# RWKV-6 attention with an MLP on one core: r-u-k products of round 2 as tasks between MLP steps, GpSimd's chain there one slot earlier, and the first MLP's second products in runs of three

## The chip, the cores and the metric

The kernel runs on one core of a Trainium2 chip. Its time is the device time in microseconds, the median over runs. A core has TensorE (PE, matrix products, with a weight load PEld beside it), VectorE (DVE), ScalarE (ACT), GpSimd (POOL) and SyncE, whose queue (SPq) issues nearly all DMAs here. Each engine works through its own instructions in order and waits for semaphores of the others.

## The reference

Four batches, eight heads of 48, 768 steps. An RWKV-6 recurrence runs over the steps, and its output, with the heads side by side (384 wide), goes through a layer norm and an MLP (384 to 1536 to 384) with a residual:

```python
for t in range(S):
    cur = np.einsum('bhd,bhe->bhde', u[None] * kt, vt)
    y[:, :, t] = np.einsum('bhd,bhde->bhe', rt, state + cur)
    state = wt[:, :, :, None] * state + np.einsum('bhd,bhe->bhde', kt, vt)
...
xn = (x - mu) / np.sqrt(var + 1e-06) * g_ln
ch = np.maximum(xn @ w_ch1, 0.0) @ w_ch2
return x + ch
```

The step's own term, `r . (u * k)` times `v`, is what the code calls the r-u-k product: `own_products` multiplies r, k and u, `own_sums` sums over a head's 48 numbers, `own_term` multiplies the sums with v.

## The kernel before

**Rounds, units, levels.** The work is cut into 8 rounds (4 batches, 2 halves of 384 steps). A round has two units of four heads each, so round 2 has units 4 and 5, and round 3 has units 6 and 7. Within a round the recurrence is solved in six levels (`lev` 0 to 5) that double the span each time. A level of a unit is `quads` (PE, products of r and k into `a_ps`), then `grow` (DVE, multiplies r and k by decays, `rkT<-rkT,tot` or `rkT<-rkT,wT`) and `keep` (DVE, into `A`). Level 5 is followed by `ends` (PE transposes `kn_ps`, ACT copies `kn`). In the next round `states` makes `kv` on PE and `s` on DVE, `exchanged` copies `sx` on ACT, and `outputs` makes `y` on PE and adds `vo` on DVE into `x`.

**The MLP beside it.** The MLP of a finished round is a generator, `mlp`, of 24 steps: 12 make a block of the hidden layer each (`h_ps` on PE, `h` on ACT), 12 make parts of the second product (`o_ps`), with three products to a step. When a block's 12 products are done, DVE adds `x` into `o` and a DMA writes it. PSUM has two buffers (`ps_m`) for `h_ps` and `o_ps` together. The first MLP takes its first two blocks of rows together (`groups`), all others one after another. Its weights are converted on the way: `begin` (ACT), `shifted` and `added` (DVE) handle 24 parts, and `converted(n)` makes sure that n parts are issued.

**The order.** The loop over `rnd` and `lev` is the written order of all work. Each (`rnd`, `lev`) is a slot, `slot = (rnd - 1) * NLEV + lev`. A slot does some work at once and collects the rest in `tasks`. `fill(UNTIL[slot], tasks)` then spreads the tasks evenly among the MLP steps up to the number `UNTIL[slot]`: with m tasks and n steps, a step follows whenever (i + 1) * n // m grows. PE, ACT, DVE and POOL (all wrapped in `InOrder`) keep the written order. So does `SPO` on the DMA queue, where an instruction is pinned behind the one written just before it on that queue; plain `SP` instructions may be moved ahead when their inputs are ready and a buffer is free.

**The operations around the change.** From round 3 on the units take the level-0 term another way: `load_before` fetches k and v one step earlier into the two old `nat_w` buffers (`i` 0 for k, 1 for v), `own_products` multiplies that k by r as well (`nat_w<-nat_w,nat_r`), `own_sums` sums it too (`next`), and `own_term` has three multiplications for one. `stage` loads `w_runs`, `k_runs` and `r_runs` into a ring of four raw buffers, `squares` transposes them on DVE. `totals` makes products of decays (`tot`, `decay`), on POOL for the rounds spoken of here. The product tile `rk` has one buffer, which `own_products` fills and `own_sums` frees. All operations of the compute engines show as L49 in the profile, since a helper records them; the DMA queue's lines are those of `load` (L125), `stage` (L163), `load_before` (L174), `load_v` (L186), `load_vx` (L192) and the write of `out` (L743).

Of the kernel before, what the change touches and what calls it, by code (L numbers as in the profile page):

```python
# [52 lines left out]
def kernel(  # L53
# [19 lines left out]
    P = 128  # L73
# [11 lines left out]
    NLEV = 6  # L85
# [243 lines left out]
    def converted(n):  # L329
        while joined < n:  # L330
            join()
# [377 lines left out]
    def mlp(rnd):  # L709
        b, f0 = rounds[rnd]  # L710
        x, xT, name = xs[b, f0], xTs[rnd], f"{b}_{f0}"
        hs = []
        for f in range(FC):
            converted(KC * (f * P // WC + 1))
            ps = ps_m.tile([P, RN], F32, tag="m", name=f"h_ps{name}_{f}")
            for kc in range(KC):
                PE.matmul(
                    ps, w1_sb[:, kc, ts(f, P)], xT[:, kc, :], start=kc == 0, stop=kc == KC - 1
                )
            hs.append(ph.tile([P, RN], F32, tag="h", name=f"h{name}_{f}"))  # L720
            ACT.activation(out=hs[f], in_=ps, func=AF.Relu)
            yield

        groups = ((0, 1), (2,)) if rnd == 0 else ((0,), (1,), (2,))
        at = 0
        for group in groups:
            ps = {
                i: ps_m.tile([P, H, D], F32, tag="m", name=f"o_ps{name}_{i}") for i in group
            }
            for f in range(FC):  # L730
                converted(len(parts) - FC + f + 1)
                for i in group:
                    PE.matmul(
                        ps[i].rearrange("p h d -> p (h d)"), hs[f][:, ts(i, P)],
                        w2_sb[:, f, :], start=f == 0, stop=f == FC - 1,
                    )
                    at += 1
                    if at % KC == 0 and f < FC - 1:
                        yield
            for i in group:  # L740
                o = p2.tile([P, H, D], F32, tag="o", name=f"o{name}_{i}")
                DVE.tensor_tensor(out=o, in0=ps[i], in1=x[:, i], op=ALU.add)
                SP.dma_start(  # L743
                    out=out[b, ds(f0 * RN + i * P, P), :].rearrange("t (h d) -> t h d", d=D),
                    in_=o,
                )
            yield
# [36 lines left out]
    def each(f, *ranges):  # L784
        calls = [()]
        for r_ in ranges:
            calls = [c + (x,) for c in calls for x in r_]
        return [lambda c=c: f(*c) for c in calls]
# [8 lines left out]

    FIRST = 3
    odd = const.tile([P, 1], F32, name="odd")

    def take(eng, q):

        own_products(q, eng)
        own_sums(q)


    (u0, u1), new = units_of(0), units_of(1)
# [91 lines left out]
    for rnd in range(1, NR + 1):  # L899
        old, now, new = units_of(rnd - 1), units_of(rnd), units_of(rnd + 1)  # L900
        if rnd == 1:
            old = []
        for lev in range(NLEV):
            slot = (rnd - 1) * NLEV + lev
            if rnd == 2:

                for q in old if lev < 2 else []:
                    (states, outputs)[lev](q)
                    if lev or q == old[-1]:
                        mlp_step()  # L910
            elif old and lev < 2 * U:
                (states if lev < U else outputs)(old[lev % U])
                if lev >= U and now:
                    mlp_step()
            for q in now:
                if slot and (lev or rnd < FIRST):
                    quads(q, lev)
            for which in ("rk",) if lev < NLEV - 1 else "kr":
                for q in now:
                    grow(q, lev, which)  # L920
            if now:
                if rnd == 1 and lev == 0:
                    totals(rnd, DVE)
                keep(rnd, lev)
            tasks = []
            if rnd == 1:
                if lev < 2:
                    tasks += each(load, new, "kr"[lev], [SPO])
                if lev == 2:
                    SPO.dma_start(  # L930
                        out=u_bc,
                        in_=bass.AP(
                            tensor=u.tensor, offset=u.offset, ap=[[0, P], [D, H], [1, D]]
                        ),
                    )
                    tasks += each(load_v, now, [SPO])
                if lev == 3:
                    tasks += each(load_vx, now, [SPO])
                if lev in (4, 5):
                    own_term(now[lev - 4], POOL)  # L940
            if rnd == 2 and lev == 0:
                tasks += each(load_v, now)
                DVE.tensor_reduce(
                    out=odd, in_=ident.rearrange("p (q two) -> p q two", two=2)[:, :, 1],
                    axis=AX.X, op=ALU.add,
                )
            if rnd == 2 and lev == 2:
                for q in now:
                    take(DVE, q)
                    tasks += each(load, new[q % U :][:1], "kr")  # L950
            if rnd == 2 and lev in (3, 4):
                tasks += each(own_term, now[lev - 3 :][:1], [POOL])
            if rnd > 2 and lev == 1:
                tasks += each(load, new, ["kr"])
            first = 3 if rnd == 2 else 1
            if rnd > 1 and new and first - 1 <= lev < first + 3:
                m = lev - first
                turns = [(new, "w"), (new[:1], "kr"), (new[1:], "kr")]
                if m >= 0:
                    tasks += each(squares, *turns[m], pairs)  # L960
                if m < 2:
                    tasks += each(stage, *turns[m + 1], pairs)
            if rnd == 2:
                if lev == 0:
                    tasks += each(exchanged, old)
                if lev == 1:
                    tasks += [lambda: moments(1), lambda: norm(1)]
                if lev == 2:
                    tasks += each(turned_x, [1], range(KC))
            elif old and lev < U:  # L970
                tasks += each(exchanged, [old[lev]])
            if lev == 3 and rnd > 1:
                for q in now:
                    load_vx(q)
                for q in new:
                    load_v(q)
                if new:
                    load_before(new[0], k, 0)
                    load_before(new[0], v, 1)
                if rnd > 2:  # L980
                    moments(rnd - 1)
                    tasks = each(norm, [rnd - 1]) + tasks
            if lev == 4 and rnd > 2:
                tasks += each(turned_x, [rnd - 1], range(KC))
            if lev == 4 and rnd > 1:
                tasks += each(own_products, new[:1], [POOL])
            if lev == NLEV - 1:

                if now:
                    mlp_step()  # L990
                if rnd >= 2 and new:
                    own_sums(new[0])
                if rnd >= 2:
                    tasks += each(load_before, new[1:], [k], [0])
                    tasks += each(own_term, new[:1], [POOL])
                    tasks += each(load_before, new[1:], [v], [1])
                    tasks += each(own_products, new[1:], [POOL])
                    tasks += each(own_sums, new[1:]) + each(own_term, new[1:], [POOL])
                    if new:
                        tasks += each(totals, [rnd + 1], [POOL])  # L1000
                if now:
                    tasks = mixed(
                        tasks,
                        each(ends, now, pairs) + each(finish, [2, 2, 4])
                    )
                if rnd == 1:
                    tasks = [join] * JOINS[lev] + tasks + each(totals, [rnd + 1], [POOL])
            if rnd == 1 and lev < NLEV - 1:

                n = (1, 2, 2, 1, 0, 0)[lev] * NP  # L1010
                tasks += mixed(
                    [begin] * BEGINS[lev], [join] * JOINS[lev], ahead[:n],
                    each(product_sums, now) if lev == 1 else [],
                )
                del ahead[:n]
            fill(UNTIL[slot], tasks)
            if lev == (2 if rnd == 2 else 4) and old:
                mlps.append(mlp(rnd - 1))
# [32 lines left out]
```

## Time and profile before

| | us |
|---|---|
| median of 9 runs | 565.66 |
| lowest and highest | 563.68 and 567.8 |
| the profiled execution, its own time | 566.1 |
| its span in the profile | 564.4 |
| TensorE busy in it | 547.2 (97%) |
| VectorE, ScalarE, GpSimd busy | 332.1, 168.8, 133.6 |

The span covers the instructions; the device time has 1.7 us more around them. A line of a timeline gives the start and the length in us, the engine, the operation, what it writes and reads, shapes, how many were merged, and in brackets the idle time before it with what ended it. Small matrix products are pipelined, so a busy TensorE need not be TensorE at its peak. The granted clock is the share of TensorE's full clock that it was given. A product of full precision is two records on PE.

### The profile page before, as it was taken

Reading aid. Unit: us, or ns where it says so; the run is one execution under the profiler, and the core shown is the slowest. Engines: PE = TensorE matmul, PEld = TensorE weight load, DVE = VectorE, ACT = ScalarE, POOL = GpSimd, SP = SyncE. Lnnn points to the kernel's source line nnn. Section 1 sums busy time; section 2 is a strip of 40 time slices with the busy share of each in tenths; the row PEclk is TensorE's granted clock in tenths of the full one; section 3 lists DMA queues with packets and bytes.
Section 4 is the critical chain, followed back from the end, with each engine's and each line's share of the span. In section 5 each row is a group of like instructions: output and inputs, shape, how many; then the busy total and the mean of one; then the engine's idle time right before and its main releaser. Section 6 shows DMA issues by size and latency. Waiting matters only on the chain.

```text
span 564.4 us, 18202 instructions
## 1 busy us (share of the span) xinstructions
PE 547.2 (97%) x7898; PEld 358.5 (64%) x7898; DVE 332.1 (59%) x654; ACT 168.8 (30%) x363; POOL 133.6 (24%) x157
## 2 busy tenths in 40 slices
PE   8999998998889999999999999999999999999997
PEld 6776665665555666666666666666666666665554
DVE  4889998769767785757386655666572611130000
ACT  3576877502250015201421026201521025202200
POOL 6040010205184019301590029021640000000000
PEclk9899999999997999999999999999999999999999
DMA  9948887245466464636463546545200000000000
GB/s 233 194 127 168 189 218 185 57 95 100 131 150 140 123 130 118 133 113 141 96 138 100 134 113 140 115 120 116 58 1 2 31 15 1 2 29 15 0 15 28
DMA packets 141552, 56.64 MB, mean 100 GB/s; under 512 B 124448, under 2 KB 130720, under 8 KB 141472
## 3 DMA queue, kind: packets, MB, share of 16 engines
q1 hardware_dynamic: 139600, 54.88, 41.9%
q8 instruction: 62, 1.02, 0.7%
q10 hardware_dynamic: 1872, 0.59, 0.4%
q14 instruction: 18, 0.15, 0.1%
HBM read 48.66 MB, written 4.72 MB: 95 GB/s over the span
## 4 chain that ended last, share of the span: by engine, by line
PE 82%; DVE 8%; ACT 3%; DMA 2%; issue 2%; SPq 1%; POOL 0%; DVEq 0%; ACTq 0%; POOLq 0%
PE o_ps L49 33%; PE h_ps L49 27%; PE a_ps L49 9%; PE y L49 4%; DVE rkT L49 3%; DVE w_sb L49 2%; PE kv L49 2%; PE kn_ps L49 2%; ACT rest L49 1%; DMA nat_r<-in_r_dram 1%; PE xT_ps L49 1%; PE own_ps L49 1%; PE k_ps L49 1%; PE r_ps L49 1%; DVE A L49 1%
## 5 line engine op out<-in xcount | busy, mean ns | idle before, releaser
L49 PE MATMUL o_ps<-w_sb,h 128*128 128x384 f32 x576 | 199.8, 496 | 1.0 <-ACT h L49 1.0
L49 PE MATMUL h_ps<-xT,w_sb 128*128 128x384 f32 x576 | 196.4, 491 | 2.6 <-DVE o L49 1.4
L49 PEld LDWEIGHTS h_ps<-xT,w_sb 128*128 128x128 f32 x576 | 105.6, 190 | 70.4 <-DVE o L49 2.0
L49 PEld LDWEIGHTS o_ps<-w_sb,h 128*128 128x128 f32 x576 | 106.4, 192 | 67.6 <-ACT h L49 2.3
L49 DVE TENSOR_TENSOR rkT<-rkT,tot 128x768 f32<-128x768 f32 (+1 forms) x96 | 77.4, 847 | 27.8 <-issue 17.6
L49 ACT ACTIVATE h<-h_ps 128x384 f32<-128x384 f32 x96 | 46.9, 488 | 142.6 <-PE h_ps L49 142.4
L49 PEld LDWEIGHTS a_ps<-rkT 48*64 48x64 f32 x4128 | 65.7, 136 | 24.2 <-issue 13.1
L49 PE MATMUL a_ps<-rkT 48*64 48x32 f32 x4128 | 70.9, 221 | 4.0 <-DVE rkT L49 3.9
L49 DVE TENSOR_TENSOR o<-o_ps,x 128x384 f32<-128x384 f32 x24 | 13.3, 555 | 95.8 <-PE o_ps L49 95.7
L49 POOL TENSOR_TENSOR vo<-v,own 128x576 f32<-128x576 f32 x16 | 19.5, 1223 | 104.5 <-DVE own L49 62.2
L49 ACT ACTIVATE rstd<-mv,eps 128x3 f32<-128x3 f32 x8 | 2.4, 296 | 133.5 <-DVE mv L49 133.5
L49 DVE SCALAR_TENSOR_TENSOR s<-s,decay,kv 128x48 f32<-128x48 f32 x160 | 29.3, 258 | 18.9 <-PE kv L49 18.9
L49 POOL TENSOR_TENSOR nat_w<-nat_w,nat_r 128x576 f32<-128x576 f32 x10 | 14.4, 1436 | 102.8 <-DMA nat_w<-in_v_dram 101.8
L49 DVE COPY_PREDICATED A<-mask,a_ps 128x768 f32<-128x768 int8 x32 | 38.3, 1198 | 0.0
L49 DVE TENSOR_TENSOR x<-y,vo 128x288 f32<-128x288 f32 x32 | 13.2, 453 | 35.4 <-PE y L49 35.4
L49 ACT ACTIVATE xT<-xT_ps,g_sb 128x384 f32<-128x384 f32 x24 | 13.6, 579 | 48.4 <-PE xT_ps L49 48.4
L49 DVE TENSOR_TENSOR rkT<-rkT,wT 128x768 f32<-128x768 f32 x16 | 24.9, 1590 | 0.9 <-PE a_ps L49 0.8
L49 DVE TENSOR_REDUCE own<-rk 128x12 f32<-128x576 f32 x12 | 9.0, 750 | 23.2 <-POOL rk L49 23.2
L49 DVE TENSOR_SCALAR w_sb<-w_sb 128x384 f32<-128x384 f32 (+1 forms) x48 | 20.4, 425 | 0.8
L49 DVE STREAM_TRANSPOSE rkT<-r_runs 128x384 f32<-128x384 f32 x20 | 15.6, 841 | 3.7 <-DMA r_runs<-in_r_dram 3.7
L49 PEld LDWEIGHTS y<-v,A 64*64 64x64 f32 x384 | 12.8, 134 | 7.6 <-issue 4.4
L49 POOL TENSOR_TENSOR tot<-wT 128x768 f32<-128x768 f32 x6 | 12.4, 2072 | 20.7 <-DVE rkT L49 20.7
(88 smaller groups left out, 541.1 us busy)
## 6 DMA issues: line engine op xcount, KB each, us to landing
raw<-in_moe_w_ch_dram SPq DMA_DIRECT2D x24, 384.0 KB, 3.8
w_runs<-in_w_dram SPq DMA_DIRECT2D x79, 70.0 KB, 2.0
k_runs<-in_k_dram SPq DMA_DIRECT2D x79, 70.0 KB, 1.9
r_runs<-in_r_dram SPq DMA_DIRECT2D x79, 70.0 KB, 2.0
v<-in_v_dram SPq DMA_DIRECT2D x48, 96.0 KB, 2.9
out_dram<-o SPq DMA_DIRECT2D x24, 192.0 KB, 2.5
nat_r<-in_r_dram SPq DMA_DIRECT2D x42, 96.0 KB, 3.3
nat_k<-in_k_dram SPq DMA_DIRECT2D x42, 96.0 KB, 3.4
```

The costliest lines, as they stand in the source:

```text
L49: return lambda *args, **kw: self.tc.keep_in_program_order(f(*args, **kw))
```

## The change

It has three parts. In the first MLP the second products of two row blocks no longer alternate from product to product: three products of one block run, then three of the other. In round 2, level 2, the r-u-k products and sums of units 4 and 5 become tasks in front of the loads that overwrite their inputs, and the loads of unit 6's shifted k and v and of v are written there, the shifted ones through the pinned queue. And in round 2 POOL's chain for units 6 and 7 is written one level earlier: unit 6's products in level 3, its sums and term and unit 7's products in level 4, where they were in levels 4 and 5. For later rounds the chain's code is shared and its order kept.

```diff
-        at = 0
         for group in groups:
...
-            for f in range(FC):
-                converted(len(parts) - FC + f + 1)
+            for f0_ in range(0, FC, KC):
+                converted(len(parts) - FC + f0_ + KC)
                 for i in group:
-                    PE.matmul(
-                        ps[i].rearrange("p h d -> p (h d)"), hs[f][:, ts(i, P)],
-                        w2_sb[:, f, :], start=f == 0, stop=f == FC - 1,
-                    )
-                    at += 1
-                    if at % KC == 0 and f < FC - 1:
+                    for f in range(f0_, f0_ + KC):
+                        PE.matmul(
+                            ps[i].rearrange("p h d -> p (h d)"), hs[f][:, ts(i, P)],
+                            w2_sb[:, f, :], start=f == 0, stop=f == FC - 1,
+                        )
+                    if f < FC - 1 or i != group[-1]:
                         yield
...
-    def take(eng, q):
-
-        own_products(q, eng)
-        own_sums(q)
...
             if rnd == 2 and lev == 2:
                 for q in now:
-                    take(DVE, q)
+                    tasks += each(own_products, [q], [DVE]) + each(own_sums, [q])
                     tasks += each(load, new[q % U :][:1], "kr")
+            if rnd == 2 and lev == 2:
+                tasks += each(load_before, new[:1], [k], [0], [SPO]) + each(load_v, new)
+                tasks += each(load_before, new[:1], [v], [1], [SPO])
             if rnd == 2 and lev in (3, 4):
                 tasks += each(own_term, now[lev - 3 :][:1], [POOL])
...
             if lev == 3 and rnd > 1:
                 for q in now:
                     load_vx(q)
-                for q in new:
-                    load_v(q)
-                if new:
-                    load_before(new[0], k, 0)
-                    load_before(new[0], v, 1)
                 if rnd > 2:
+                    for q in new:
+                        load_v(q)
+                    if new:
+                        load_before(new[0], k, 0)
+                        load_before(new[0], v, 1)
                     moments(rnd - 1)
                     tasks = each(norm, [rnd - 1]) + tasks
             if lev == 4 and rnd > 2:
                 tasks += each(turned_x, [rnd - 1], range(KC))
-            if lev == 4 and rnd > 1:
+
+            chain = 3 if rnd == 2 else 4
+            if rnd > 1 and new and lev == chain:
                 tasks += each(own_products, new[:1], [POOL])
+            if rnd > 1 and new and lev == chain + 1:
+                if lev < NLEV - 1:
+                    tasks += each(own_sums, new[:1])
+                else:
+                    own_sums(new[0])
+                tasks += each(load_before, new[1:], [k], [0])
+                tasks += each(own_term, new[:1], [POOL])
+                tasks += each(load_before, new[1:], [v], [1])
+                tasks += each(own_products, new[1:], [POOL])
             if lev == NLEV - 1:
 
                 if now:
                     mlp_step()
-                if rnd >= 2 and new:
-                    own_sums(new[0])
                 if rnd >= 2:
-                    tasks += each(load_before, new[1:], [k], [0])
-                    tasks += each(own_term, new[:1], [POOL])
-                    tasks += each(load_before, new[1:], [v], [1])
-                    tasks += each(own_products, new[1:], [POOL])
                     tasks += each(own_sums, new[1:]) + each(own_term, new[1:], [POOL])
                     if new:
                         tasks += each(totals, [rnd + 1], [POOL])
```

## The prediction

> **What bounds the kernel now.** I read the page first, then the time TensorE (PE) waited, then the chain of waits and the timelines of PE, VectorE (DVE), GpSimd (POOL) and the DMA queue (SPq) between 86 and 176 us, where both edits lie.
>
> ```profile
> span 564.4 us, 18202 instructions
> PE 547.2 (97%) x7898; PEld 358.5 (64%) x7898; DVE 332.1 (59%) x654; ACT 168.8 (30%) x363; POOL 133.6 (24%) x157
> ```
> PE is busy for 97% of the span: a gain can only come out of the 17 us in which it idles, or out of stretches in which it runs slowly. From 182 to 400 us the table by stretches shows it busy all the time, so whatever is won before 182 reaches the end whole.
>
> The first idle piece is in the first MLP, where its second products (`o_ps`) begin (PE's timeline):
> ```profile
> 87.86 2.20 PE L49 MATMUL h_ps<-xT,w_sb 128*128 128x384 f32 x6 [0.50 <-ACT h L49]
> 90.13 0.91 PE L49 MATMUL o_ps<-w_sb,h 128*128 128x384 f32 x2
> 92.01 3.49 PE L49 MATMUL o_ps<-w_sb,h 128*128 128x384 f32 x10 [0.97 <-ACT h L49]
> ```
> One product is two records. The first product of block 0 runs; the first of block 1 writes the other PSUM buffer, which ScalarE (ACT) has still to empty of the last `h_ps`: 0.97 us.
>
> The second idle region is the end of round 2 (PE's timeline again):
> ```profile
> 149.20 2.20 PE L49 MATMUL h_ps<-xT,w_sb 128*128 128x384 f32 x6
> 152.66 0.87 PE L49 MATMUL kn_ps<-ident,rkT 128*128 128x128 f32 x6 [1.25 <-DVE rkT L49]
> 165.63 0.91 PE L49 MATMUL kv<-v,kn 64*64 64x48 f32 x48
> 168.81 0.90 PE L49 MATMUL a_ps<-rkT 48*64 48x32 f32 x48 [2.27 <-DVE rkT L49]
> 170.86 1.50 PE L49 MATMUL a_ps<-rkT 48*64 48x32 f32 x48 [1.15 <-DVE rkT L49]
> ```
> PE waits for DVE three times. The 2.27 and 1.15 us are slack: work that PE does later before them costs nothing until they are used up. Behind them PE runs at half clock (stretches; the column after POOL's is the granted clock):
> ```profile
> 166.00:170.00 4.00, 1.44 (x87) 1.24 (x77) 4.00 (x9) 1.24 (x3) 3.91 (x3) 0.98 0.55 157
> 170.00:173.00 3.00, 2.14 (x49) 1.87 (x50) 2.89 (x12) 0.00 (x0) 2.62 (x5) 0.50 0.55 103
> 173.00:176.00 3.00, 3.00 (x6) 1.69 (x5) 3.00 (x7) 0.86 (x2) 0.40 (x2) 0.50 0.87 165
> 176.00:179.00 3.00, 3.00 (x9) 1.67 (x8) 3.00 (x5) 0.00 (x0) 2.57 (x2) 0.89 0.74 143
> ```
> The 18 `o_ps` records from 172.37 take 8.16 us in the chain of waits; 18 such records take 6.00 from 242.50. The half clock costs 2.16 us.
>
> What sets DVE there (timelines of DVE, SPq and POOL):
> ```profile
> 151.36 0.85 DVE L49 STREAM_TRANSPOSE rkT<-r_runs 128x384 f32<-128x384 f32 x1 [0.94 <-DMA r_runs<-in_r_dram]
> 152.07 1.92 DVE L49 TENSOR_TENSOR rkT<-rkT,tot 128x384 f32<-128x384 f32 x4
> 153.91 0.74 DVE L49 TENSOR_REDUCE own<-rk 128x12 f32<-128x576 f32 x1
> 155.83 1.55 DVE L49 STREAM_TRANSPOSE rkT<-k_runs 128x384 f32<-128x384 f32 x2
> 161.59 0.75 DVE L49 TENSOR_REDUCE own<-rk 128x12 f32<-128x576 f32 x1 [0.79 <-POOL rk L49]
> 164.03 0.75 DVE L49 TENSOR_REDUCE next<-nat_w 128x12 f32<-128x576 f32 x1 [1.69 <-POOL nat_w L49]
> ```
> ```profile
> 153.51 3.96 SPq L163 DMA_DIRECT2D r_runs<-in_r_dram  x8
> 157.58 2.22 SPq L174 DMA_DIRECT2D nat_w<-in_k_dram  x3
> ```
> ```profile
> 162.57 1.43 POOL L49 TENSOR_TENSOR nat_w<-nat_w,nat_r 128x576 f32<-128x576 f32 x1 [1.01 <-DMA nat_w<-in_k_dram]
> ```
> DVE's last wait (164.03) is for POOL, POOL's is for the shifted k of unit 7, and that load stands behind 32 DMAs that SPq issues back to back from 141.35.
>
> **Runs of three.** The instructions are the same, three to a step. Block 1's first product moves behind three of block 0: 90.13 + 3 x 0.65 (1.94 for a step) = 92.07, against 92.01 when its buffer is free. The 0.97 us go. The step now needs the third converted part at once; by 90 us DVE has joined 18 parts and the step needs 15, the later steps 18, 21 and 24 at about 96, 103 and 107, joined by 88.8, 95.8 and 103.7. No new wait. From 92 to 119.55 PE waits only once more (0.30, for ACT), and `grow` at 120.58 waits for PE; from there DVE, SPq and DMA hang on one another. So all of it moves: -0.97. Bounds: 0 if DVE's conversions (no idle over 0.52 us from 83 to 103) took over, -0.97 otherwise; I take -0.97, since each row above leaves room.
>
> **Round 2's products between steps.** In slot 8 the list has 19 tasks and three MLP steps, and a step comes after tasks 7, 13 and 19. All four tasks on DVE are among the first six, and the only DVE operation of the three steps (the `o` add at 135.46) is in the last: DVE's order is what it was, so 0, and the 1.37 us that PE waits for this `o` at 136.07 stay. The loads of k and r wait for the same products as before: 0.
>
> **Unit 6's shifted loads.** They are issued at 55 to 58 (k) and at 66.6 and 103 (v) before; now k is pinned behind the r load of unit 7, whose last DMA is issued at 136.71. SPq is idle from 138.01 to 141.35; three such DMAs take 1.55: they fit. Landing: the same kind takes 2.9 us at the median, so about 141. POOL now runs unit 6's products before `vo` of unit 5: they need r of unit 6 (about 136), so 136.2 to 140.2, then the shifted product to 142.7; before, 142.36. `vo` of unit 5 (1.15) moves behind, beside `grow` at 143.24: up to +1.2 us on DVE (a 0.96 multiply took 2.16 beside POOL at 137.5), which DVE's waits for DMAs (1.10, 0.93, 0.94) hide; if they were gone it would cost all of it. The early loads' place at 55 to 103 frees 6 DMAs, of which no engine waits for one: 0.
>
> **POOL's chain one slot ahead.** `own_sums` of unit 6 moves from behind the four level-5 multiplies to before them, but behind the `r_runs` transposes that end at 152.21. That is 155.83 - 153.91 = 1.92 us put in front of the multiplies that PE waits for at 152.66. They then start at 153.99, beside POOL's `vo` chain, which now starts at 153. Bounds for the first of them: 0.53 alone, 1.2 at the ratio 2.16/0.96; I take 1.0 from the ratio at 135.93 (two multiplies of 0.96 in 3.74). PE's transposes: 155.0 for 152.66, +2.35; behind them 2.27 + 1.15 us of slack. DVE finishes the multiplies at about 157.6 and the four transposes at about 160.6, inside its wait of 1.86.
>
> The gain meant here does not come: the k load of unit 7 stays behind `r_runs` on SPq (its buffer comes free after the last transpose, which frees the raw buffer of the last `r_runs` first), so the shifted product stays at 162.57 and `next` at 164.03. Of DVE's waits 0.79 us merge into the 1.69. The `s` and `grow` operations keep their times, PE's `a_ps` too: 0. Rounds after 2 keep the order of every engine: 0.
>
> **The clock.** PE's idle time moves: 151.34 to 155.0 (3.7 us) for 1.25, and the 2.27 is gone. In the trace half clock came at 169.9 for 6.8 us, after a stretch with idle pieces of 2.27 and 1.15 us; pieces of 1.37 (134.7) and 1.25 (151.4) brought none. I expect it to follow the new gap in three cases of four, and not at 170, where 1.15 us is left. There it falls on work with 1.15 us of slack. If it lasts 3.4 us (as at 23 us in the trace) it costs 1.7 - 1.15 = 0.55, if 6.8, 2.25; I take 0.75 x 0.55 = +0.4, and -2.16 for the old place.
>
> [...]
>
> Sum against the profiled execution (566.1, span 564.4 and 1.7 around it; the median 565.66 lies 0.44 below): 566.1 - 0.97 - 2.16 + 0.4 = 563.4.
>
> **The rivals.** 0.3% (1.70 us) is about what a measurement of this kernel can tell; faster means below 563.96, slower above 567.36.
> - Forecast, 0.50: 563.4, its own range 562.3 to 564.9; 0.37 of it below 563.96.
> - The half clock stays as dear (two windows at the new gap, or again at 170): 566.1 - 0.97 = 565.1. For it: the 48-row products before 172 are light work. 0.22, same.
> - DVE's conversions take the 0.97 over and the clock price stays: 565.7. 0.07, same.
> - POOL's lead pays: the k load of unit 7 gets in front of `r_runs` without holding it, 0.79 + 1.69 go: 563.4 - 2.5 = 560.9. Against it: SPq's order. 0.08, faster.
> - Slower: unit 6's k load, no longer early, is queued behind `k_runs` and `r_runs` (149.71). The last of three lands about 153.9; POOL's product 1.45, DVE's reduce and scale 1.3, so the multiplies start near 157.2 and PE at 157.7: +5.0, less 2.27 of slack = +2.7, and a longer gap saves no clock: 566.1 - 0.97 + 2.7 = 567.8. It decides once that load lands later than 152.07 - 1.45 = 150.6. For it: nothing pins `k_runs` behind it. 0.13.
>
> Range 562.0 to 567.2: leaves out 0.08 below and about 0.1 above. Faster 0.45, same 0.42, slower 0.13.
>
> **What would show it.** `o_ps` opens with six records and no wait at 90. DVE's `own` stands before the four 128x384 multiplies; PE's `kn_ps` wait is 3 to 4 us; the 2.27 before `a_ps` is gone; `next` still waits for POOL and that for `nat_w`; the granted clock is 1.00 from 170 to 177. I am wrong if half clock is still there, or if `next` no longer waits.

## The result, and the profile after

The changed kernel takes 562.44 us (median of 17 runs, 559.41 to 565.13), the kernel before 566.05 in the same measurement (54 runs). The ratio is 0.9938, 95% interval 0.9921 to 0.9954: faster by 0.6%, about 3.5 us. The profiled execution took 563.73 us, its span is shorter by 2.4 us:

```profile
span 562.0 us, 18190 instructions
PE 547.3 (97%) x7898; PEld 359.4 (64%) x7898; DVE 336.0 (60%) x654; ACT 169.2 (30%) x363; POOL 136.2 (24%) x157
```

The span alone misleads here. At about 23 us, long before the first edit acts at 90 us, PE ran at half clock for 10.2 us in this execution and for 3.4 us in the one of before, and the first `o_ps` began 2.51 us later (92.64 against 90.13). So I compare by stretches between marks on PE: *o1* is the first `o_ps` of the first MLP, *M2* the first `a_ps` of round 2 at level 1, *o3* the first `o_ps` of round 3's MLP steps (before: 172.30), *y3* the first `y` of round 3. From y3 to the end of PE's last instruction, all profiles but one take 380.43 us (that one 380.54), so what differs lies ahead of y3.

| us | before | after | difference |
|---|---|---|---|
| start to o1 | 90.13 | 92.64 | +2.51 |
| o1 to M2 | 29.42 | 28.37 | -1.05 |
| M2 to o3 | 52.74 | 51.09 | -1.65 |
| o3 to y3 | 8.16 | 6.00 | -2.16 |

The first MLP, PE's timeline:
```profile
90.34 2.20 PE L49 MATMUL h_ps<-xT,w_sb 128*128 128x384 f32 x6 [0.75 <-ACT h L49]
92.64 4.14 PE L49 MATMUL o_ps<-w_sb,h 128*128 128x384 f32 x12
```
Twelve records of `o_ps` (six products) stand without a wait; the 0.97 us behind the first product are gone.

The end of round 2, PE's timeline:
```profile
155.52 1.33 PE L49 MATMUL kn_ps<-ident,rkT 128*128 128x128 f32 x6 [2.67 <-DVE rkT L49]
157.04 0.88 PE L49 MATMUL kn_ps<-ident,rkT 128*128 128x128 f32 x3 [0.18 <-DVE rkT L49]
157.71 2.84 PE L49 MATMUL h_ps<-xT,w_sb 128*128 128x384 f32 x6
...
169.86 0.92 PE L49 MATMUL kv<-v,kn 64*64 64x48 f32 x48
170.60 1.57 PE L49 MATMUL a_ps<-rkT 48*64 48x32 f32 x96
172.10 6.07 PE L49 MATMUL o_ps<-w_sb,h 128*128 128x384 f32 x18
```
Both waits before `a_ps` (2.27 and 1.15 us) are gone, the one before `kn_ps` has grown from 1.25 to 2.67, and the 18 `o_ps` are at full speed. The stretches of the same profile (the granted clock is the column after POOL's) show where the half clock went:
```profile
155.00:157.00 2.00, 1.33 (x6) 0.93 (x6) 2.00 (x4) 0.59 (x2) 1.77 (x2) 0.70 0.57 156
157.00:160.00 3.00, 2.96 (x8) 2.05 (x9) 3.00 (x2) 0.85 (x2) 2.92 (x3) 0.63 0.63 157
...
170.00:173.00 3.00, 3.00 (x147) 2.69 (x146) 2.89 (x13) 0.46 (x1) 2.59 (x5) 1.00 0.72 150
173.00:176.00 3.00, 3.00 (x11) 1.75 (x10) 3.00 (x5) 0.86 (x2) 0.00 (x0) 1.00 0.82 153
```
It begins at 155.8, lasts 3.4 us and stretches six `kn_ps` from 0.87 to 1.33 and six `h_ps` from 2.10 to 2.84.

DVE's timeline, then POOL's, then the DMA queue's:
```profile
137.38 3.02 DVE L49 TENSOR_TENSOR rkT<-rkT,tot 128x768 f32<-128x768 f32 x2
...
153.05 0.70 DVE L49 TENSOR_REDUCE own<-rk 128x12 f32<-128x576 f32 x1
...
154.92 5.33 DVE L49 TENSOR_TENSOR rkT<-rkT,tot 128x384 f32<-128x384 f32 x4
...
163.72 0.75 DVE L49 TENSOR_REDUCE next<-nat_w 128x12 f32<-128x576 f32 x1
```
```profile
138.07 1.52 POOL L49 TENSOR_TENSOR rk<-nat_k,nat_r 128x576 f32<-128x576 f32 x1 [2.47 <-DMA nat_r<-in_r_dram]
...
143.65 1.43 POOL L49 TENSOR_TENSOR nat_w<-nat_w,nat_r 128x576 f32<-128x576 f32 x1 [1.98 <-DMA nat_w<-in_k_dram]
...
162.24 1.45 POOL L49 TENSOR_TENSOR nat_w<-nat_w,nat_r 128x576 f32<-128x576 f32 x1 [0.72 <-DMA nat_w<-in_k_dram]
```
```profile
138.71 2.51 SPq L49 DMA_DIRECT2D nat_w<-in_k_dram  x3
...
142.07 3.89 SPq L163 DMA_DIRECT2D k_runs<-in_k_dram  x8
...
158.20 1.49 SPq L174 DMA_DIRECT2D nat_w<-in_k_dram  x3
```
Four things to see. The two level-3 multiplies of `grow` take 3.02 us for 3.74. `own` stands ahead of the level-5 multiplies, and these take 5.33 us for 1.92. DVE doesn't wait for POOL any more, and `next` runs at 163.72. Counted from M2, `k_runs` begins on SPq at 21.07 instead of 21.80.

### The profile page after: what moved, and what is told of

The parts are those of the page before. It is cut to its first block, busy times and chain, and to the rows that moved or that the text cites. A ratio compares the mean times of both kernels' runs of the same rounds, so it can differ in the third digit from the quotient of the medians.

```text
span 562.0 us, 18190 instructions
## 1 busy us (share of the span) xinstructions
PE 547.3 (97%) x7898; PEld 359.4 (64%) x7898; DVE 336.0 (60%) x654; ACT 169.2 (30%) x363; POOL 136.2 (24%) x157
## 3 DMA queue, kind: packets, MB, share of 16 engines
q8 instruction: 62, 1.02, 0.8%
## 4 chain that ended last, share of the span: by engine, by line
PE 85%; DVE 7%; SPq 3%; DMA 2%; ACT 2%; issue 1%; ACTq 0%; DVEq 0%
PE o_ps L49 33%; PE h_ps L49 29%; PE a_ps L49 9%; PE y L49 4%; DVE w_sb L49 3%; PE kv L49 2%; PE kn_ps L49 2%; DVE rkT L49 2%; DMA nat_r<-in_r_dram 1%; SPq L163 1%; PE xT_ps L49 1%; PE own_ps L49 1%; PE k_ps L49 1%; PE idle L49 1%; PE r_ps L49 1%
## 5 line engine op out<-in xcount | busy, mean ns | idle before, releaser
L49 PE MATMUL o_ps<-w_sb,h 128*128 128x384 f32 x576 | 197.4, 492 | 0.1
L49 DVE TENSOR_TENSOR rkT<-rkT,tot 128x768 f32<-128x768 f32 (+1 forms) x96 | 82.0, 895 | 30.7 <-issue 17.6
L49 ACT ACTIVATE h<-h_ps 128x384 f32<-128x384 f32 x96 | 46.9, 489 | 143.8 <-PE h_ps L49 143.6
L49 PE MATMUL kn_ps<-ident,rkT 128*128 128x128 f32 x96 | 14.6, 288 | 3.8 <-DVE rkT L49 2.9
L49 PEld LDWEIGHTS kn_ps<-ident,rkT 128*128 128x128 f32 x96 | 11.5, 146 | 9.5 <-DVE rkT L49 3.6
```

The source lines that it names most:

```text
L49: return lambda *args, **kw: self.tc.keep_in_program_order(f(*args, **kw))
```

## The experiments

Each kernel is read by the same marks, in one profile for each row. "Half clock" gives start and length of the stretch that falls between 150 and 180 us.

| kernel | o1 to M2 | level-3 multiplies | M2 to `k_runs` on SPq | `k_runs` to unit 7's `next` | M2 to o3 | o3 to y3 | M2 to y3 | half clock |
|---|---|---|---|---|---|---|---|---|
| before | 29.42 | 3.74 | 21.80 | 22.68 | 52.74 | 8.16 | 60.91 | 169.9, 6.8 |
| after | 28.37 | 3.02 | 21.07 | 21.65 | 51.09 | 6.00 | 57.10 | 155.8, 3.4 |
| runs of three alone | 28.40 | 3.74 | 21.80 | 22.54 | 52.44 | 7.16 | 59.61 | 172.0, 3.4 |
| all but runs of three | 29.43 | 1.82 | 21.19 | 21.65 | 51.67 | 6.00 | 57.68 | 154.2, 3.4 |
| changed, sums back | 28.39 | 3.03 | 21.08 | 22.26 | 51.60 | 8.48 | 60.08 | 167.7, 6.8 |
| before, zeros ahead of `a_ps` | 29.42 | 3.75 | 21.80 | 23.01 | 52.47 | 6.00 | 58.47 | none |
| changed, zeros ahead of `kn_ps` | 28.41 | 3.02 | 21.05 | 22.81 | 51.76 | 7.39 | 59.15 | 171.7, 3.4 |
| before, level-2 tasks and pinned loads | 29.43 | 3.74 | 21.77 | 23.09 | 52.53 | 6.00 | 58.53 | 155.1, 3.4 |
| before, unit 6's products early | 29.42 | 1.82 | 19.87 | 22.81 | 50.94 | 7.77 | 58.71 | 167.2, 6.8 |
| sums back, totals early | 28.41 | 3.03 | 21.39 | 23.35 | 51.14 | 7.64 | 58.78 | 172.6, 3.4 |
| the parts that paid, and zeros | 28.39 | 3.03 | 21.25 | 22.67 | 50.40 | 6.00 | 56.40 | none |
| changed, loads unpinned | 28.41 | 1.82 | 19.87 | 21.72 | 49.26 | 6.00 | 55.26 | none |
| the same, second profile | 28.38 | 3.03 | 21.08 | 22.79 | 51.53 | 6.00 | 57.53 | 155.2, 3.4 |
| changed, second profile | 28.38 | 1.82 | 21.24 | 21.80 | 51.39 | 6.00 | 57.39 | 155.5, 3.4 |

**Runs of three alone.** The diff's first hunk by itself, on the kernel before:

```diff
-            for f in range(FC):
-                converted(len(parts) - FC + f + 1)
+            for f0_ in range(0, FC, KC):
+                converted(len(parts) - FC + f0_ + KC)
                 for i in group:
+                    for f in range(f0_, f0_ + KC):
...
```

> Only the runs of three, the rest as before. Theory (the wait for the second PSUM buffer goes and nothing takes it over): o_ps opens without its 0.97 us wait, and the kernel gains about 1.0 us against before; half clock still falls near 170 us. Rival (DVE's conversions take it over, and all of the change's gain lies in round 2): within 0.3 us of before.

Measured: o1 to M2 is 28.40, so 1.02 us are won and kept; every kernel that has this part shows 28.4, every one without it 29.4. M2 to y3 came out 1.3 us shorter too, though no edit lies there: the half clock lasted 3.4 us instead of 6.8. By the runs the median is 564.45 against 565.85, ratio 0.9989 (0.9968 to 1.001), which cannot tell 1 us from nothing. The stretch can.

**All but the runs of three.** The changed kernel with the old loop over `f` and `i`:

```diff
-            for f0_ in range(0, FC, KC):
-                converted(len(parts) - FC + f0_ + KC)
+            for f in range(FC):
+                converted(len(parts) - FC + f + 1)
                 for i in group:
-                    for f in range(f0_, f0_ + KC):
...
```

> Only round 2's part (tasks, pinned loads, GpSimd's chain one slot ahead), the second products alternate as before. Theory (PE's gap moves from 167 to 152, where there is slack, and half clock with it): 2 to 3 us faster than before, kn_ps waits about 3 us, no half clock near 170. Rival (the gain is the runs of three and little else): within 0.5 us of before.

Measured: 563.53 against 565.85, ratio 0.9965 (0.9943 to 0.9988). The half clock behind `a_ps` is gone and one of 3.4 us is at 154.2. Round 2's part is the larger one.

**Changed, but unit 6's sums back behind the level-5 multiplies.**

```diff
-            if rnd > 1 and new and lev == chain + 1:
-                if lev < NLEV - 1:
-                    tasks += each(own_sums, new[:1])
-                else:
-                    own_sums(new[0])
+            if rnd > 1 and new and lev == NLEV - 1:
+                own_sums(new[0])
```

> The changed kernel, but the sums of unit 6 and what follows them stand behind the level-5 multiplies again; unit 6's products, the pinned loads and the runs of three stay. Theory (the gain of round 2 is the place of PE's gap): kn_ps waits about 1.3 us again, a_ps about 2 and 1 us near 167, half clock falls behind them; 1.5 to 2.5 us slower than the changed kernel. Rival (the gain is in the loads and in unit 6's products beside less DVE work): as fast as the changed kernel or up to 0.5 us faster, since PE no longer waits 3 us for kn_ps.

Measured: 563.52 against 565.85, ratio 0.996 (0.9936 to 0.9984). The waits and the half clock are back (PE's timeline and the stretches):
```profile
166.02 0.90 PE L49 MATMUL a_ps<-rkT 48*64 48x32 f32 x48 [1.69 <-DVE rkT L49]
168.07 1.50 PE L49 MATMUL a_ps<-rkT 48*64 48x32 f32 x48 [1.15 <-DVE rkT L49]
```
```profile
166.00:170.00 4.00, 2.83 (x97) 2.68 (x98) 3.89 (x11) 0.00 (x0) 3.69 (x5) 0.71 0.60 130
170.00:173.00 3.00, 3.00 (x6) 1.49 (x5) 3.00 (x8) 0.86 (x2) 0.27 (x2) 0.50 0.89 168
```
M2 to y3 is 60.08, close to before. The runs alone don't show it: against the changed kernel (ratio 0.9938) the difference is about 1.2 us, where 1.5 to 2.5 were expected, and the two intervals overlap. But M2 to o3 is still 1.14 shorter than before: something else in the change gains there, and it isn't the sums.

**Before, with zeros in the gap ahead of `a_ps`.** `warm(9, "t")` issues three 128x384 products of zeros into a spare PSUM buffer.

```diff
+            if rnd == 3 and lev == 1:
+                warm(9, "t")
             for q in now:
                 if slot and (lev or rnd < FIRST):
```

> The kernel before with three idle products (zeros, 128x384, 0.65 us each, read by nobody) in PE's gap behind the second kv of round 3. Theory (the gap costs by the half clock behind it): the idle piece of 2.27 us shrinks to about 0.3, no half clock near 170, about 2 us faster than before. Rival (half clock is drawn by the light 48-row products, or falls at random): half clock still there in most runs, 0 to 0.3 us slower than before.

Measured: 562.89 against 565.85, ratio 0.9975 (0.995 to 0.9999). PE's timeline and the stretches:
```profile
164.66 2.21 PE L49 MATMUL idle<-nought 128*128 128x384 f32 x6
167.09 0.90 PE L49 MATMUL a_ps<-rkT 48*64 48x32 f32 x48 [0.22 <-DVE rkT L49]
```
```profile
166.00:170.00 4.00, 2.54 (x99) 1.75 (x97) 3.89 (x5) 0.50 (x2) 3.84 (x4) 1.00 0.65 148
170.00:173.00 3.00, 3.00 (x20) 1.84 (x13) 3.00 (x14) 0.86 (x2) 1.28 (x4) 1.00 0.79 148
```
With the gap filled, and nothing else changed, no half clock comes at 170 and `o_ps` takes 6.00 us. The runs say that this is no chance of one profile: the mean granted clock of an execution is 0.997 or more in 7 of these 12 runs, and in none of the 80 runs of before that were timed in the experiments (0.994 at most). So the clock's 2.16 us could be had without moving any real work; by the ratio of the runs the gain is about 1.4 us (0.1 to 2.8).

**Changed, with zeros in the gap ahead of `kn_ps`.**

```diff
                 if now:
                     mlp_step()
+                if rnd == 2:
+                    warm(9, "t")
```

> The changed kernel with three idle products (zeros, 128x384, read by nobody) in PE's new gap before kn_ps. The stretch from unit 4's level-1 products of round 2 to the first y of round 3 is 57.10 us in the changed kernel. Theory (PE and DVE come to the first o_ps of round 3 together, so half clock at 155 costs nothing): no half clock near 155, a new wait of 0.5 to 1.5 us before a_ps, stretch 56.9 to 57.4. Rival (half clock there costs the end): stretch 55.9 to 56.5.

Measured: 565.29 in one run, against a median of 566.56 of before. Neither expectation: the half clock at 155 went, and one came at 171.7, behind a single wait of 1.15 us:
```profile
171.17 1.13 PE L49 MATMUL a_ps<-rkT 48*64 48x32 f32 x48 [1.15 <-DVE rkT L49]
172.23 7.47 PE L49 MATMUL o_ps<-w_sb,h 128*128 128x384 f32 x18
```
```profile
170.00:173.00 3.00, 1.85 (x52) 1.50 (x50) 2.89 (x10) 0.00 (x0) 2.69 (x5) 0.78 0.73 144
173.00:176.00 3.00, 3.00 (x8) 1.66 (x7) 3.00 (x8) 0.86 (x2) 0.89 (x3) 0.65 0.94 172
```

**Before, with the level-2 tasks and the pinned loads only.**

```diff
-                    take(DVE, q)
+                    tasks += each(own_products, [q], [DVE]) + each(own_sums, [q])
...
+            if rnd == 2 and lev == 2:
+                tasks += each(load_before, new[:1], [k], [0], [SPO]) + each(load_v, new)
+                tasks += each(load_before, new[:1], [v], [1], [SPO])
```

> The kernel before with only the tasks of level 2 and the pinned loads; GpSimd's chain and the second products as before. Stretch as above, 60.91 us in the kernel before. Theory (the loads' place and the tasks are worth nothing): k_runs starts 21.8 us after the stretch's start as before, stretch 60.0 to 61.5 with half clock near 170. Rival (the later loads relieve the queue): stretch under 59.8 with half clock.

Measured: M2 to `k_runs` 21.77 for 21.80, and M2 to o3 52.53 for 52.74: tasks and loads by themselves do nothing, as forecast. One run took 565.34. The stretch of 58.53 misses the forecast of 60.0 to 61.5, because the half clock fell at 155.1 here, on the work ahead of slack. It came behind a longer wait than in before (2.06 us for 1.25):
```profile
155.03 2.41 PE L49 MATMUL kn_ps<-ident,rkT 128*128 128x128 f32 x9 [2.06 <-DVE rkT L49]
```
That fits the other profiles: half clock came at 154 to 156 in all five in which PE waited 2.06 us or more there, and in none of the nine with 1.42 or less. The waits of 0.58 and 1.15 before `a_ps` drew none here.

**Before, with unit 6's products on POOL one level earlier only.**

```diff
-            if lev == 4 and rnd > 1:
+            if rnd > 1 and new and lev == (3 if rnd == 2 else 4):
                 tasks += each(own_products, new[:1], [POOL])
```

> The kernel before with only GpSimd's products of unit 6 one level earlier (in front of the term of unit 5). [...]

Measured: 563.86 in one run; M2 to o3 is 1.80 us shorter, by this one line, and `k_runs` starts 1.93 sooner, where I had put 0.6 to 0.8 and the changed kernel has 0.73. DVE's timeline, POOL's and the DMA queue's:
```profile
135.90 1.82 DVE L49 TENSOR_TENSOR rkT<-rkT,tot 128x768 f32<-128x768 f32 x2
```
```profile
136.75 2.23 POOL L49 TENSOR_TENSOR rk<-nat_k,nat_r 128x576 f32<-128x576 f32 x1 [2.64 <-DMA nat_k<-in_k_dram]
```
```profile
139.39 3.58 SPq L163 DMA_DIRECT2D k_runs<-in_k_dram  x8
```
The same in the kernel before, DVE, POOL and the DMA queue:
```profile
135.93 3.74 DVE L49 TENSOR_TENSOR rkT<-rkT,tot 128x768 f32<-128x768 f32 x2
```
```profile
135.63 1.15 POOL L49 TENSOR_TENSOR vo<-v,own 128x576 f32<-128x576 f32 x1 [1.48 <-DMA nat_r<-in_r_dram]
136.82 2.04 POOL L49 TENSOR_TENSOR rk<-nat_k,nat_r 128x576 f32<-128x576 f32 x1
```
```profile
141.35 3.59 SPq L163 DMA_DIRECT2D k_runs<-in_k_dram  x8
```
There POOL starts unit 5's `vo` 0.30 us ahead of the first level-3 multiply, and unit 6's product right behind it; both multiplies are slowed, to 1.67 and 2.16 us, 3.74 in all. With unit 6's products written first, POOL itself waits for their loads, and the first multiply takes 0.95 (profile of after; the second 2.16). What the two take went with how soon POOL's product came: in the ten profiles with this order, POOL's product starts 0.61 to 0.82 us after the first multiply in the six with 3.02 or 3.03 us, and 0.85 to 1.03 in the four with 1.82. In the first group POOL's product takes 1.40 to 1.60, in the second 2.06 to 2.25: the time is lost on DVE in the one and on POOL in the other. Why the two engines slow each other no trace here shows.

**Sums back, and the decay products early.** Round 3's `totals` (12 small products on POOL) are written behind unit 5's `own_term` in level 4, so that the level-0 multiplies of round 3 don't run beside them.

```diff
+            if rnd == 2 and lev == 4:
+                tasks += each(totals_early, [3], [POOL])
...
-                    if new:
+                    if new and rnd > 2:
                         tasks += each(totals, [rnd + 1], [POOL])
```

> A version meant to beat both: the changed kernel with unit 6's sums behind the level-5 multiplies again, and round 3's products of decays made by GpSimd right after the term of unit 5 in level 4, in tiles of the weight conversion that are free by then (12 instructions of half size for 6). Theory (the two level-0 multiplies of round 3 take 3.77 us only because GpSimd's totals run beside them, and PE has no long gap then): they take about 1.9, kn_ps waits under 1.3 us, no half clock near 170, stretch 54.9 to 56; 1 to 2 us faster than the changed kernel, some 561. Rival (PE's gap before a_ps stays, and half clock with it): stretch 57 to 59, no faster than the changed kernel.

Measured: 564.23 against 566.56, ratio 0.9952 (0.9922 to 0.9981); the two level-0 multiplies take 2.49 us for 3.77, a part of what was expected (about 1.9), but `next` comes later (23.35 us after `k_runs`), PE still waits 2.40 us and the half clock stays at 172.6. The stretch, 58.78, is within what one program's profiles differ by; the rival was nearer.

**The parts that paid, together.** Runs of three, unit 6's products early, the totals early, and zeros ahead of `a_ps`; sums, loads and level 2 as before. Against the kernel before, with the runs of three and `totals_early` as above:

```diff
-            if lev == 4 and rnd > 1:
+            if rnd > 1 and new and lev == (3 if rnd == 2 else 4):
                 tasks += each(own_products, new[:1], [POOL])
...
+            if rnd == 2 and lev == 4:
+                tasks += each(totals_early, [3], [POOL])
...
+            if rnd == 3 and lev == 1:
+                warm(9, "t")
```

> A version meant to beat both, from what the runs so far showed: the kernel before with the runs of three, GpSimd's products of unit 6 one level earlier (loads and sums where they were), round 3's products of decays right behind the term of unit 5, and three idle products in PE's gap before a_ps of round 3. Theory (all parts add up, since they sit on one chain of DVE, queue and DMA, and the gap no longer costs the clock): level-3 multiplies 1.8 to 3.0 us, level-0 multiplies of round 3 about 2.5 us, stretch from unit 4's level-1 products to the first y of round 3 55.3 to 56.5 us (changed kernel 57.10), full clock behind it; median 1 to 2 us under the changed kernel. Rival (the gap that opens sooner is not covered, or GpSimd's totals push its other work): stretch 57 to 59, no faster than the changed kernel.

Measured: 561.18 against 566.63, ratio 0.9894 (0.9864 to 0.9924), in the same comparison as the changed kernel's second measurement (562.81, ratio 0.9934, 0.9909 to 0.9959). It is the fastest that was timed; the two intervals overlap.
```profile
165.99 2.21 PE L49 MATMUL idle<-nought 128*128 128x384 f32 x6
168.13 1.60 PE L49 MATMUL a_ps<-rkT 48*64 48x32 f32 x96
```
The zeros take the whole gap, and no half clock falls between 30 and 560 us.

**The changed kernel again,** with no edit.

> The changed kernel once more, beside the version above on one chip. Theory: 0.9938 of before within 0.003; half clock in the profile falls between 153 and 161 and not between 165 and 180. Rival (where half clock falls is chance): half clock behind 165.

Measured: the gain repeats (ratio above). But the path differs: level-3 multiplies of 1.82 us, and yet `k_runs` no earlier (DVE's timeline, the DMA queue's):
```profile
136.72 1.82 DVE L49 TENSOR_TENSOR rkT<-rkT,tot 128x768 f32<-128x768 f32 x2
...
139.34 2.90 DVE L49 STREAM_TRANSPOSE wT<-w_runs 128x384 f32<-128x384 f32 x4
```
```profile
138.06 2.72 SPq L49 DMA_DIRECT2D nat_w<-in_k_dram  x3
140.87 0.59 SPq L742 DMA_DIRECT2D out_dram<-o  x1
141.58 3.91 SPq L163 DMA_DIRECT2D k_runs<-in_k_dram  x8
```
The transposes that free `k_runs`' raw buffers begin 1.2 us earlier than with 3.02, but SPq is busy with the pinned shifted k until 140.78 and the `out` behind it.

**Changed, with unit 6's shifted k and v and the v loads back in level 3, unpinned.** Run once, and then timed.

```diff
-            if rnd == 2 and lev == 2:
-                tasks += each(load_before, new[:1], [k], [0], [SPO]) + each(load_v, new)
-                tasks += each(load_before, new[:1], [v], [1], [SPO])
...
+                for q in new:
+                    load_v(q)
+                if new:
+                    load_before(new[0], k, 0)
+                    load_before(new[0], v, 1)
                 if rnd > 2:
-                    for q in new:
-                        load_v(q)
-                    if new:
-                        load_before(new[0], k, 0)
-                        load_before(new[0], v, 1)
```

> The changed kernel with unit 6's shifted loads and v loads where they were before (unpinned, written in level 3). Theory (the pinned loads stand in front of k_runs and out on the queue and hold GpSimd's shifted product up): that product needs no wait near 143, k_runs starts 19.8 to 21.1 us after the stretch's start for 21.07, stretch 55.9 to 57.1 at full clock. Rival (the pinned loads are free or help): 21.1 or later and 57.1 or more.

> The changed kernel with unit 6's shifted and v loads back where the kernel before has them, run again and timed. Theory: the loads put between the out store and k_runs cost the changed kernel some 1.8 us, by moving k_runs and the shifted product, and so the gap in which half clock falls: from the first level-1 products of round 2 to the first y of round 3 again 55.3 to 56.0 us (the changed kernel 57.1 and 57.4, the kernel before 60.91), and a median of 560.3 to 561.3 us where the kernel before has 566.1, a ratio of 0.987 to 0.992. Rival: the 558.79 of the one look was a run without the early half clock, and the loads cost little: a ratio of 0.993 to 0.995, as the changed kernel, and a stretch of 56.8 to 57.5 us.

Measured: the first run took 558.79, with M2 to y3 55.26. The timed runs gave 563.64 against 567.51, ratio 0.9931 (0.99 to 0.9962), the changed kernel's own gain, with two of eight runs at 560.1 and the rest at 563.3 to 564.1; the second profile has 57.53. The rival of the second expectation was right: one program, two profiles, 2.27 us apart, and the first alone would have put 1.8 us on the pins. The lines say how. In the first, POOL's product came 1.03 us behind the multiply and DVE took 1.82:
```profile
134.27 1.82 DVE L49 TENSOR_TENSOR rkT<-rkT,tot 128x768 f32<-128x768 f32 x2
```
In the second profile it came 0.69 behind, DVE took 3.03, and unit 7's shifted k landed late:
```profile
137.29 3.03 DVE L49 TENSOR_TENSOR rkT<-rkT,tot 128x768 f32<-128x768 f32 x2
...
164.78 0.75 DVE L49 TENSOR_REDUCE next<-nat_w 128x12 f32<-128x576 f32 x1 [1.72 <-DMA w_runs<-in_w_dram]
```
(DVE's wait is put down to another DMA; POOL's shifted product, which `next` reads, started at 163.33 after 2.39 us of waiting for its k.) What the pinned loads cost is therefore only partly known: nothing where the multiplies take 3.02 (`k_runs` at 21.05 to 21.08 with the pins, 21.08 without), 1.3 to 1.4 where they take 1.82 (21.19 and 21.24 with them, 19.87 and 19.87 without). The two kernels with the totals early stand apart: 21.39 with the pins and 21.25 without, at 3.03.

## Why the prediction was right, and where it was not

The forecast was 563.4 us and faster; measured were 562.44 and -3.5 us where the sum had -2.7. The first two terms held, the bigger miss lies in a term of nothing. That the total came so near is in part luck: from M2 to o3 the profile shows -1.65 where the sum had +0.4.

**Runs of three, -0.97.** Right: -1.05 in the profile, -1.02 alone. DVE's conversions did not take over.

**The clock, -2.16 and +0.4.** Right in the outcome. `o_ps` takes 6.00 us in all five profiles that have unit 6's sums ahead and no zeros; in the six without either, the half clock was there in five and at 155 once. The new place cost 0.6: `o_ps` starts 0.89 us behind the end of the level-0 multiplies where PE waited for them (171.55 to 172.44 in the second profile with loads unpinned), so in the profile of after, where these end at 170.57, it could have started at 171.46 and started at 172.10. I had 0.55 at three in four. The runs show that half clock was mostly moved, not removed: over 28 runs of the changed kernel the mean granted clock is 0.991, over 80 of before 0.989. At equal clock nearly the whole gain is still there: at 0.988 a mean of 563.2 us in 6 runs against 566.5 in 19, at 0.994 560.9 in 4 against 564.3 in 23. Two steps were weaker than they read. "Not at 170, where 1.15 us is left" did not hold: the run with zeros ahead of `kn_ps` drew it with just these 1.15 us, where level 2's tasks and pinned loads alone had 0.58 and 1.15 and drew none. In the profile of after PE comes late, at 170.6, as the multiplies end at 170.57, so that not even the 1.15 is left. And the run with the `a_ps` gap filled shows that the gain was not tied to the move.

**"Round 2's products between steps", 0, and "unit 6's shifted loads", 0.** Alone they are nothing, as said (21.77 for 21.80). The step that failed is the next sentence of the second: "`vo` of unit 5 moves behind, beside `grow`: up to +1.2 us on DVE". I costed what `vo` would meet in its new place and not what it left. It left the level-3 multiplies, whose 3.74 us I had read only as a ratio for other rows. Taking it from there is worth 0.72 us or 1.92, and `k_runs` follows, since the transposes behind those multiplies free its buffers: -0.73 in the profile of after. The cost in level 4 is real, 1.97 us (3.75 for 1.78) where I had at most 1.2, and hidden, as said: DVE's three waits for DMAs behind it shrank from 2.97 us in all to 1.44.

**"The gain meant here does not come."** Half wrong: `next` no longer waits for POOL in the profile of after, which the prediction had named as a sign of being wrong. From `k_runs` to `next` of unit 7 it is 22.68 before and 21.65 after, 1.03 less. The sum is short. DVE's waits of 1.86, 0.79 and 1.69 us in that stretch are gone, 4.34 in all. The level-5 multiplies take 3.41 more (5.33 against 1.92, where I had about 3.6 in all from the ratio). 4.34 - 3.41 = 0.93, and small differences make up the rest. POOL does run ahead now, and DVE pays most of that back in multiplies that run beside it. It needs the k load to land in time, and "stays at 162.57" was wrong there: the load still stands behind `r_runs`, but its three DMAs took 1.49 us to issue for 2.22. It came as early in four of the six profiles with the sums ahead (`next` at 21.65 to 21.80) and not in the other two (22.79 and 22.81). The kernels with the sums behind have 22.26 to 23.35. Why an issue now and then takes 0.7 to 1.2 us longer (2.22, 2.51 and 2.72 for three DMAs of shifted k that elsewhere took 1.49) stayed open.

**The multiplies' price.** +2.35 for `kn_ps` was nearly right: counted from `k_runs` it starts 13.45 us later for 11.31, +2.14. From M2 it is +1.41, since `k_runs` itself starts 0.73 earlier. PE's wait there was 2.67 us, less than the 3 to 4 named as a sign; with the sums ahead and no zeros it was 1.10 to 2.90.

So -1.65 from M2 to o3 is -0.73 (level 3), -1.03 (`next`) and +0.11 for the rest (in it the second `a_ps` of 1.50 us at half clock, 0.6 less now, and the new half clock, 0.6 more), where the sum had +0.4. The profiled stretches add to -4.86 us without the early half clock, more than the -3.5 of the runs: two profiles of one program differ by up to 2.3 us there, and the kernel before has one profile only. The runs give the size, the stretches the places.

**The rivals.** The clock as dear as before (6.8 us of half clock at the new gap, or again at 170: 565.1): shown wrong by five profiles. POOL's lead (560.9): 1.0 of its 2.5 us came. The late k load (567.8): unit 6's `nat_w` landed at 143.6, well before the 150.6 from which it would decide.

## What to carry to other kernels

When a step moves, price the place it leaves as carefully as the place it goes to: a VectorE operation that takes twice its usual time beside GpSimd (here 2.16 us for 0.95) is a term of the sum, not just a ratio. Where PE drops to half clock behind a gap, try filling the gap with products of zeros before reordering real work (here the 18 `o_ps` behind it took 6.00 us for 8.16). Compare marks inside the trace when one profile's span carries a disturbance from elsewhere, and take two profiles of one program before a difference of 2 us is explained.

## What the hardware showed that I had not expected

- **Half clock came in pieces of about 3.4 us, and it differed between executions.** Lengths of 3.4, 6.8 and 10.2 were seen: 3.4 at 23.1 us and 6.8 at 169.9 in the profile of before, 10.2 at 22.7 and 3.4 at 155.8 in that of after, and the ones at 23 lie far ahead of the first edit. One program (loads unpinned) had a mean granted clock of 1.0 in one execution and 0.987 in another, and its first `o_ps` started at 89.49 and 92.53. Little idle time was enough once: in the run with zeros ahead of `kn_ps`, 1.15 us of waiting among the small products of `a_ps` were followed by half clock at 171.7. How long a gap has to be to draw it, these runs do not settle.
- **Behind products of zeros the clock stayed full.** 2.2 us of them ahead of `a_ps` did it in the kernel before (`o_ps` 6.00 us for 8.16), and no half clock came there in the version of the parts that paid.
- **A few hundredths of a microsecond went with 1.2 us.** With POOL's product 0.82 us behind the first of two DVE multiplies, these took 3.03 us and the product 1.40 (sums back); with 0.85 they took 1.82, and the product 2.23 and 2.25 (unit 6's products early; the changed kernel's second profile). Short multiplies of 0.48 us (1.92 for four) grew to 1.33 in a series beside POOL (5.33 for four).
